# Loading batch 0 as token pairs and turning u of the first two batches on the tensor engine, in a fused retention and low-rank MLP kernel

## The chip, the cores and the metric

The kernel runs on one core of one Trainium2 chip. The metric is the device time in microseconds (us) of one execution; times are medians of the runs in the fast state. The engines are PE (matmul), DVE (vector), ACT (scalar), POOL (GpSimd) and SP (which here only issues loads). ACT and POOL issue DMAs too: ACT the transposing ones, POOL the weights and the stores.

## The reference, cut to what matters

```python
# q, k, v: (4 batches, 8 heads, 768 tokens, 64)
for t in range(S):                                  # retention, gamma per head
    state = gamma * state + k[:, :, t] (x) v[:, :, t]
    y[:, :, t] = scale * q[:, :, t] @ state
x  = y as (4, 768, 512)                             # heads side by side
u  = x + (x^T @ U @ V)^T                            # rank 32, along the tokens
out = u + relu(u @ w_ch1) @ w_ch2                   # 512 -> 2048 -> 512
```

The low-rank step mixes all 768 tokens of a batch, so u of a batch exists only when its whole attention is done. The MLP of batch b can start only then.

## The kernel before

The attention is computed in 128-token chunks with a state carried from chunk to chunk, in bf16. The matmuls of the MLP of batch b−1 are the carpet: they are issued in order, and pieces of the attention of batch b are woven in at marks, given as fractions of that MLP's cost.

```python
AT = {1: at(0.56, 0.052, 0.026), 2: at(0.09, 0.105, 0.05)}   # first chunk, step, score-to-mix
LR = {1: (0.87, 0.89, 0.905, 0.905), 2: (0.71, 0.75, 0.83, 0.89)}
for b in range(1, B):
    ...
    marks.append((s_at, part(score4, b, ci)))
    marks.append((m_at, part(mix4, b, ci)))
    ...
    marks += zip(LR[w], (mixed, part(lr_expand, b, 0, 4), part(lr_turn, b, 0),
                         part(lr_turn, b, 2)))
    weave(mlp_pieces(b - 1), marks)
```

The first MLP product needs u with the channels on the partitions (uT). `lr_turn` makes it, with DMAs that transpose, issued by ACT. (Only the first 512 tokens of batch 0 are made on PE directly.)

```python
def lr_turn(b, j0):
    for j in (j0, j0 + 1):
        nc.scalar.dma_start(out=uTs[b][:, :, ts(j, P)], in_=us[b][:, j],
                            transpose=True)
```

All loads of q, k and v go through SP in one fixed order. Batch 0 comes in 18 loads of 256 KB, one per tensor and 128-token chunk, in rows of 64 floats (256 B). After the gate below, which waits for the last w1 weights, the loads of the later batches follow.

```python
src[b, :, ts(ci, P), :].rearrange("h p d -> p h d")       # batch 0: 256 B packets
...
gate = rinT.tile([P, 2, NCK, 256], fp32, tag="kin", name="gate")
nc.gpsimd.tensor_copy(out=gate[:1, 0, 0, :1], in_=w1b[:1, 0, DH - 1:])
```

POOL casts the arrived tiles (`ki`, `qi`, `kd`, `vd`) and also issues the stores of the output, in program order. Three output tiles `o_sb` are in use in turn: DVE may write one only when the store of three tiles before has read it.

## Time and profile before

| | before |
|---|---|
| time, median | 263.67 us (263.1 to 264.25) |
| span of the profiled run, PE busy | 261.8 us, 224.0 us |
| first matmul of MLP 0 / 1 / 2 / 3 | 35.24 / 104.51 / 157.80 / 213.22 us |

From the profile's page: engine totals, then the busy tenths of PE and its granted clock in 40 slices of 6.5 us each, then the queue of the loads (q1) and of the transposes (q10) with packets, MB and share of the 16 DMA engines' time.

```profile
span 261.8 us, 5299 instructions
PE 224.0 (86%) x2224; PEld 120.4 (46%) x2224; DVE 102.6 (39%) x193; ACT 77.5 (30%) x172; POOL 95.1 (36%) x130
...
PE   0686789939999980999999996799999998999991
...
PEclk9999999988999997799999999799999999999997
...
q1 hardware_dynamic: 59520, 22.02, 44.9%
...
q10 hardware_dynamic: 10880, 2.62, 6.5%
```

PE is the engine that matters. It loses its time in the first five slices, in slice 9, in slice 16, and around slice 25, and PEclk drops behind the last three of these holes. The waits of PE in the timeline (start, length, line and operation, count, and in brackets the idle time before it with its releaser) say what the holes are:

```profile
35.24 3.15 PE L395 MATMUL mlp<-uT,w1b 128*128 128x512 bf16 x7 [0.68 <-ACT uT L75]
...
56.44 8.81 PE L395 MATMUL mlp<-uT,w1b 128*128 128x256 bf16 x64 [4.26 <-DMA uT<-u]
...
104.51 1.86 PE L395 MATMUL mlp<-uT,w1b 128*128 128x512 bf16 x4 [7.20 <-DMA uT<-u]
```

PE stood still for 4.26 and 7.20 us for transposes. The four 512-column matmuls after the second wait took 1.86 us, 0.47 each, where a warm one takes 0.22 (32 of them in 7.08 us from 45.10 us): half speed. The first line shows that the MLP begins at 35.24 us, also at half speed. (PEclk reads 9 there all the same, so this half speed is read from the durations alone.)

### The profile page before, as it was taken

Reading aid. Unit: us, or ns where it says so; the run is one execution under the profiler, and the core shown is the slowest. Engines: PE = TensorE matmul, PEld = TensorE weight load, DVE = VectorE, ACT = ScalarE, POOL = GpSimd, SP = SyncE. Lnnn points to the kernel's source line nnn. Section 1 sums busy time; section 2 is a strip of 40 time slices with the busy share of each in tenths; the row PEclk is TensorE's granted clock in tenths of the full one; section 3 lists DMA queues with packets and bytes.
Section 4 is the critical chain, followed back from the end, with each engine's and each line's share of the span. In section 5 each row is a group of like instructions: output and inputs, shape, how many; then the busy total and the mean of one; then the engine's idle time right before and its main releaser. Section 6 shows DMA issues by size and latency. Waiting matters only on the chain.

```text
span 261.8 us, 5299 instructions
## 1 busy us (share of the span) xinstructions
PE 224.0 (86%) x2224; PEld 120.4 (46%) x2224; DVE 102.6 (39%) x193; ACT 77.5 (30%) x172; POOL 95.1 (36%) x130
## 2 busy tenths in 40 slices
PE   0686789939999980999999996799999998999991
PEld 0475534428545430345754442346744443584440
DVE  5431324503465460466534501755543542331221
ACT  2555333415234200255541001256611013450000
POOL 4897900021993111979014436761000110000110
PEclk9999999988999997799999999799999999999997
DMA  8999999999919969889998189900002342001211
GB/s 163 218 210 172 174 192 217 238 196 201 191 43 208 269 119 189 165 223 171 206 211 138 54 170 256 245 3 5 3 4 78 106 125 52 0 0 44 80 66 54
DMA packets 77544, 35.72 MB, mean 136 GB/s; under 512 B 62544, under 2 KB 75984, under 8 KB 77520
## 3 DMA queue, kind: packets, MB, share of 16 engines
q1 hardware_dynamic: 59520, 22.02, 44.9%
q0 software_dynamic: 7120, 10.73, 17.5%
q10 hardware_dynamic: 10880, 2.62, 6.5%
q8 instruction: 17, 0.28, 0.5%
q14 instruction: 7, 0.06, 0.1%
HBM read 30.90 MB, written 6.29 MB: 142 GB/s over the span
## 4 chain that ended last, share of the span: by engine, by line
PE 33%; issue 31%; DMA 13%; SPq 6%; DVE 6%; POOL 6%; ACTq 3%; ACT 1%; POOLq 0%; DVEq 0%
PE mlp L395 15%; PE mlp L418 10%; DMA uT<-u 8%; SPq L133 6%; DMA in<-in_v_dram 4%; ACTq L376 3%; POOL out_dram L384 2%; DVE u L369 2%; PE r L334 2%; DMA out_dram<-o 2%; PE r L301 2%; DVE a L307 1%; PE r L325 1%; POOL vd L88 1%; PE st L286 1%
## 5 line engine op out<-in xcount | busy, mean ns | idle before, releaser
L395 PE MATMUL mlp<-uT,w1b 128*128 128x512 bf16 (+1 forms) x512 | 94.6, 341 | 17.3 <-DMA uT<-u 12.5
L418 PE MATMUL mlp<-w2b,gT 128*128 128x512 bf16 x384 | 88.0, 380 | 0.0
L395 PEld LDWEIGHTS <-w1b 128*128 128x128 bf16 x512 | 50.2, 101 | 54.0 <-issue 17.7
L402 ACT ACTIVATE gT<-mlp 128x512 bf16<-128x512 f32 (+1 forms) x88 | 42.4, 490 | 101.4 <-PE mlp L395 93.3
L418 PEld LDWEIGHTS <-gT 128*128 128x128 bf16 x384 | 35.5, 98 | 40.1
L384 POOL DMA_DIRECT2D out_dram<-o x24 | 13.4, 558 | 79.6 <-DVE o L423 79.6
L400 DVE TENSOR_SCALAR gT<-mlp 128x512 bf16<-128x512 f32 (+1 forms) x40 | 22.2, 555 | 44.2 <-PE mlp L395 44.0
L423 DVE TENSOR_TENSOR o<-mlp,u 128x512 f32<-128x512 f32 x24 | 16.6, 690 | 47.3 <-PE mlp L418 34.6
L307 DVE TENSOR_TENSOR a<-r,mask 128x512 bf16<-128x512 f32 x36 | 23.2, 686 | 17.2 <-PE r L301 15.4
L88 POOL TENSOR_TENSOR qi<-qin,gqT 128x512 bf16<-128x512 f32 x18 | 18.8, 1047 | 20.4 <-DMA qin<-in_q_dram 20.4
L86 POOL CAST ki<-kin 128x512 bf16<-128x512 f32 x18 | 13.5, 762 | 30.0 <-DMA kin<-in_k_dram 30.0
L88 POOL TENSOR_TENSOR vd<-in,gk 128x512 bf16<-128x512 f32 x18 | 18.6, 1040 | 14.1 <-DMA in<-in_v_dram 12.3
L369 DVE TENSOR_TENSOR u<-r,x 128x512 bf16<-128x512 f32 (+1 forms) x16 | 14.5, 951 | 14.7 <-PE r L362 14.7
L75 ACT ACTIVATE x<-r 128x256 bf16<-128x256 f32 x36 | 11.9, 381 | 27.4 <-PE r L334 25.6
L501 DVE TENSOR_TENSOR a<-r,mask 128x512 bf16<-128x512 f32 x12 | 7.7, 687 | 16.1 <-PE r L496 16.1
L75 ACT ACTIVATE qkT<-qk 128x1024 bf16<-128x1024 bf16 x6 | 6.1, 1024 | 10.8 <-PE qk L472 10.8
L86 POOL CAST kd<-in 128x512 bf16<-128x512 f32 x12 | 7.3, 610 | 4.2 <-DMA in<-in_k_dram 3.9
L470 PE MATMUL qk<-ident,qd 128*128 128x128 bf16 x24 | 3.7, 310 | 5.7 <-DVE ident L179 5.7
L301 PE MATMUL r<-qT,kT 32*128 32x128 bf16 x288 | 7.4, 221 | 0.9 <-DVE qT L251 0.9
L251 DVE STREAM_TRANSPOSE kT<-ki 128x256 f32<-128x256 f32 x18 | 7.8, 436 | 0.0
L251 DVE STREAM_TRANSPOSE qT<-qi 128x256 f32<-128x256 f32 x18 | 7.3, 406 | 1.0 <-POOL qi L88 1.0
L88 POOL TENSOR_TENSOR qd<-in,gq 128x512 bf16<-128x512 f32 x6 | 6.3, 1058 | 3.2 <-DMA in<-in_q_dram 3.2
(68 smaller groups left out, 129.2 us busy)
## 6 DMA issues: line engine op xcount, KB each, us to landing
in<-in_v_dram SPq DMA_DIRECT2D x24, 256.0 KB, 5.4
out_dram<-o POOLq DMA_DIRECT2D x24, 256.0 KB, 2.6
in<-in_k_dram SPq DMA_DIRECT2D x18, 256.0 KB, 5.2
kin<-in_k_dram SPq DMA_DIRECT2D x12, 384.0 KB, 7.7
qin<-in_q_dram SPq DMA_DIRECT2D x12, 384.0 KB, 12.1
w1b<-in_moe_w_ch_dram POOLq DMA_DIRECT2D x4, 512.0 KB, 8.1
w2b<-in_moe_w_ch_dram POOLq DMA_DIRECT2D x4, 512.0 KB, 17.3
in<-in_q_dram SPq DMA_DIRECT2D x6, 256.0 KB, 5.3
```

What stands on the lines that cost most here:

```text
L75: nc.scalar.activation(dst, src, AF.Copy)
L86: e.tensor_copy(out=dst, in_=src)
L88: e.tensor_tensor(dst, src, scale, op=ALU.mult)
L133: nc.sync.dma_start(out=t.rearrange("p (h d) -> p h d", h=H), in_=src)
L307: nc.vector.tensor_tensor(a[:, ds(4 * g, 4)].rearrange("p (n i) m -> p n i m", n=2), R[g][:, :, :256].rearrange("p n (i m) -> p n i m", i= ...
L369: nc.vector.tensor_tensor(v4(us[b][:, ds(j0, nj), e]), R[g][:, :, :nj * P].rearrange("p c (j e) -> p c j e", j=nj), v4(xs[b][:, ds(j0, nj) ...
L384: nc.gpsimd.dma_start(out=dst, in_=src)
L395: nc.tensor.matmul(g_p[:, :sz], w1b[:, c, ts(m, P)], uTs[b][:, c, ds(lo, sz)], start=(c == 0), stop=(c == NCB - 1))
L400: nc.vector.tensor_relu(gT[:, m, ds(lo, sz)], g_p[:, :sz])
L402: nc.scalar.activation(gT[:, m, ds(lo, sz)], g_p[:, :sz], AF.Relu)
L418: nc.tensor.matmul(ch, gT[:, m, ts(j, P)], w2b[:, m], start=(m == 0), stop=(m == NM - 1))
L423: nc.vector.tensor_tensor(o_sb, ch, us[b][:, j], op=ALU.add)
```

## The change

It has three parts:

1. *The start.* Batch 0 is loaded in blocks of 256 tokens, two neighbouring tokens in one row of 128 floats (packets of 512 B). Each block is worked as two chunks of 128 tokens (64 pairs) on the two halves of the partitions. Constants that only batch 1 needs are made later.
2. *The turns.* u of batches 0 and 1 is turned on PE (a matmul with the identity) and copied out by ACT; batches 2 and 3 keep the DMA.
3. *The marks.* Batch 1's attention and low-rank step are put later in MLP 0 and closer together, because the DMA's latency no longer has to be covered (10.0 to 12.6 us from issue to landing for the two transposes of batch 0's u, in the kernel before).

```diff
+    def load_early(nm, B0):
+        src = {"q": q, "k": k, "v": v}[nm][0, :, ds(256 * B0, 256), :].rearrange(
+            "h (t j) d -> t h (j d)", j=2)
+        ...                                   # k, q: one DMA of 512 KB; v: two of 256 KB
...
     def lr_turn(b, j0):
-        for j in (j0, j0 + 1):
-            nc.scalar.dma_start(out=uTs[b][:, :, ts(j, P)], in_=us[b][:, j],
-                                transpose=True)
+        if b > 1:
+            for j in (j0, j0 + 1):
+                nc.scalar.dma_start(out=uTs[b][:, :, ts(j, P)], in_=us[b][:, j],
+                                    transpose=True)
+            return
+        r = R[j0 // 2 % 2]
+        for c in range(NCB):
+            for jj in range(2):
+                nc.tensor.matmul(r[:, c // 2, ds(256 * (c % 2) + P * jj, P)],
+                                 us[b][:, j0 + jj, ts(c, P)], ident, start=True,
+                                 stop=True)
+        evac("A", uTs[b][:, :, ds(j0 * P, 2 * P)],
+             r.rearrange("p n (c t) -> p (n c) t", c=2))
...
-    with tc.tile_pool(name="psum0", bufs=1, space=bass.MemoryType.PSUM) as psum0:
-        ...                                   # six chunks: prep_first, turn0, mix0, score0
+    cast_early("k", 0, "DD")                  # D, P: on DVE, on POOL
+    cast_early("q", 0, "PD")
+    turn_early("k", 0)
+    turn_early("q", 0)
+    cast_early("v", 0, "PP")
+    ...                                       # three blocks, score_early, state_early, mix_early
+    cast_early("v", 2, "PD")
+    ...
+    late_consts()
...
-    AT = {1: at(0.56, 0.052, 0.026), 2: at(0.09, 0.105, 0.05)}
-    LR = {1: (0.87, 0.89, 0.905, 0.905), 2: (0.71, 0.75, 0.83, 0.89)}
+    AT = {1: at(0.74, 0.028, 0.014), 2: at(0.09, 0.105, 0.05)}
+    LR = {1: (0.91, 0.93, 0.95, 0.965), 2: (0.71, 0.75, 0.83, 0.89)}
```

More of the change, by code (lines that the diff above doesn't have):

```diff
@@ L39 @@
     RING = 19
-    NST = 4
+    NST = 3
     NLO = LO // P
@@ L59 @@
     BANKS = {"st": 1, "mlp": 3}
-    R = [psum.tile([P, 2, 512], fp32, tag="r0", name="r0")]
+    R = [psum.tile([P, 2, 512], fp32, tag=f"r{g}", name=f"r{g}") for g in range(2)]
     def bank(tag, dtype=fp32):
         n_bank[0] += 1
-        if tag in ("qk", "o"):
-            return psum0.tile([P, 2048 // (4 if dtype == fp32 else 2)], dtype,
-                              tag=tag, name=f"{tag}_{n_bank[0]}", bufs=1)
         return psum.tile([P, 2048 // (4 if dtype == fp32 else 2)], dtype,
@@ L101, in feed_natural @@
     def feed_natural(nm, b, ci):
-        src = {"q": q, "k": k, "v": v}[nm]
+        src = {"k": k, "v": v}[nm]
         feed.append(((nm, b, ci),
@@ L137, in take @@
         return ready.pop(key)
-    for ci in range(NCK):
-        for nm in "qkv":
-            feed_natural(nm, 0, ci)
     for b in range(1, B):
@@ L147 @@
             feed_natural("v", b, ci)
-    pos = consts.tile([P, NCK, H], fp32)
-    nc.gpsimd.iota(pos, pattern=[[P, NCK], [0, H]], base=0, channel_multiplier=1,
-                   allow_small_or_imprecise_dtypes=True)
-    srange = consts.tile([P, 1], fp32)
-    nc.gpsimd.iota(srange, pattern=[[0, 1]], base=0, channel_multiplier=1,
-                   allow_small_or_imprecise_dtypes=True)
-    jmat = consts.tile([P, P], fp32)
-    nc.gpsimd.iota(jmat, pattern=[[1, P]], base=0, channel_multiplier=0,
-                   allow_small_or_imprecise_dtypes=True)
+    NB = S // 256
@@ new lines @@
+    early = {}
+    kin0 = rinT.tile([P, NB, H, P], fp32, tag="kin", name="kin_0")
+    qin0 = rinT.tile([P, NB, H, P], fp32, tag="qin", name="qin_0")
+    def load_early(nm, B0):
+        src = {"q": q, "k": k, "v": v}[nm][0, :, ds(256 * B0, 256), :].rearrange(
+            "h (t j) d -> t h (j d)", j=2)
+        if nm == "v":
+            early["v", B0] = []
+            for f in range(2):
+                t = rin.tile([P, 4, P], fp32, tag="in", name=f"v0_{B0}_{f}")
+                nc.sync.dma_start(out=t, in_=src[:, ds(4 * f, 4)])
+                early["v", B0].append(t)
+        else:
+            t = (kin0 if nm == "k" else qin0)[:, B0]
+            nc.sync.dma_start(out=t, in_=src)
+            early[nm, B0] = [t[:, ds(4 * f, 4)] for f in range(2)]
@@ new lines, with ramp @@
+    for nm, B0 in ("k0", "q0", "v0", "k1", "q1", "k2", "q2"):
+        load_early(nm, int(B0))
+    n_ramp = [0]
+    def ramp(shape, pattern, mult):
+        n_ramp[0] += 1
+        t = consts.tile(shape, fp32, name=f"ramp{n_ramp[0]}")
+        nc.gpsimd.iota(t, pattern=pattern, base=0, channel_multiplier=mult,
+                       allow_small_or_imprecise_dtypes=True)
+        return t
+    srange = ramp([P, 1], [[0, 1]], 1)
+    jmat = ramp([P, P], [[1, P]], 0)
+    ident = consts.tile([P, P], bf16)
@@ new lines @@
+    nc.vector.tensor_scalar(ident, jmat, srange, None, op0=ALU.is_equal)
+    lg = [math.log(g) for g in gammas]
+    lgt = consts.tile([P, H], fp32)
+    for h in range(H):
+        nc.vector.memset(lgt[:, h:h + 1], lg[h])
+    pos2 = ramp([P, NB, H, 2], [[256, NB], [0, H], [1, 2]], 2)
+    nc.vector.tensor_tensor(
+        pos2, pos2, lgt[:, None, :, None].to_broadcast([P, NB, H, 2]), op=ALU.mult)
+    gq2 = consts.tile([P, NB, H, 2], fp32)
+    nc.scalar.activation(gq2, pos2, AF.Exp)
+    gk2 = consts.tile([P, NB, H, 2], fp32)
@@ new lines @@
+    nc.scalar.activation(gk2, pos2, AF.Exp, scale=-1.0)
+    nc.vector.tensor_scalar(gq2, gq2, 1.0 / math.sqrt(D), None, op0=ALU.mult)
+    jm2 = ramp([P, 2, P], [[-1, 2], [1, P]], 0)
+    s2 = ramp([P, 1], [[0, 1]], 2)
+    nc.vector.tensor_scalar(s2[ds(64, 64)], s2[ds(64, 64)], -128.0, None, op0=ALU.add)
+    mask2 = consts.tile([P, 2 * P], bf16)
+    nc.vector.tensor_scalar(mask2, jm2.rearrange("p j q -> p (j q)"), s2, None,
+                            op0=ALU.is_ge)
+    pos = ramp([P, NCK, H], [[P, NCK], [0, H]], 1)
@@ L159, with late_consts @@
                    channel_multiplier=4, allow_small_or_imprecise_dtypes=True)
-    feed_more()
-    lg = [math.log(g) for g in gammas]
-    for h in range(H):
-        nc.vector.tensor_scalar(pos[:, :, h], pos[:, :, h], lg[h], None,
-                                op0=ALU.mult)
-    gq = consts.tile([P, NCK, H], fp32)
-    nc.scalar.activation(gq, pos, AF.Exp)
-    gk = consts.tile([P, NCK, H], fp32)
-    nc.scalar.activation(gk, pos, AF.Exp, scale=-1.0)
-    nc.vector.tensor_scalar(gq, gq, 1.0 / math.sqrt(D), None, op0=ALU.mult)
-    for h in range(H):
-        r = ds(32 * (h // 2), 32)
-        nc.vector.tensor_scalar(
-            posT[r, :, h % 2], posT[r, :, h % 2],
-            -0.5 * math.log(D) / lg[h] - 128.0 * (h // 2), lg[h],
-            op0=ALU.add, op1=ALU.mult)
-    gqT = consts.tile([P, NCK, 2, 4], fp32)
-    nc.scalar.activation(gqT, posT, AF.Exp)
-    ident = consts.tile([P, P], bf16)
-    nc.vector.tensor_scalar(ident, jmat, srange, None, op0=ALU.is_equal)
-    mask = consts.tile([P, P], bf16)
-    nc.vector.tensor_scalar(mask, jmat, srange, None, op0=ALU.is_ge)
     states = []
     for i in range(NST):
-        t = consts.tile([P, 4, P], bf16, name=f"state{i}")
+        t = outp.tile([P, 4, P], bf16, tag="o_sb", name=f"state{i}")
         nc.vector.memset(t, 0.0)
         states.append(t)
+    mask = consts.tile([P, P], bf16)
+    gk = consts.tile([P, NCK, H], fp32)
+    gqT = consts.tile([P, NCK, 2, 4], fp32)
+    def late_consts():
+        nc.vector.tensor_scalar(mask, jmat, srange, None, op0=ALU.is_ge)
+        nc.vector.tensor_tensor(
+            pos, pos, lgt[:, None, :].to_broadcast([P, NCK, H]), op=ALU.mult)
+        nc.scalar.activation(gk, pos, AF.Exp, scale=-1.0)
+        for h in range(H):
+            r = ds(32 * (h // 2), 32)
+            nc.vector.tensor_scalar(
+                posT[r, :, h % 2], posT[r, :, h % 2],
+                -0.5 * math.log(D) / lg[h] - 128.0 * (h // 2), lg[h],
+                op0=ALU.add, op1=ALU.mult)
+        nc.scalar.activation(gqT, posT, AF.Exp)
     def causal(n):
@@ L450, in part @@
         return lambda: f(*args)
-    def prep_first(ci):
-        for nm, tag, g in (("q", "qi", gq), ("k", "kd", gk), ("v", "vd", None)):
-            t = rpre.tile([P, H, D], bf16, tag=tag, name=f"{nm}d_0_{ci}")
-            src = take(nm, 0, ci).rearrange("p (h d) -> p h d", h=H)
-            if g is not None:
-                g = g[:, ci, :, None].to_broadcast([P, H, D])
-            cast("P", t, src, g)
-            pre[nm, 0, ci] = t
-            feed_more()
-    n_state = [0]
-    def turn0(ci):
-        qd, kd, vb = (pre.pop((nm, 0, ci)) for nm in "qkv")
-        tp = bank("qk", bf16)
-        qkT = rmid.tile([P, 8, P], bf16, tag="a4", name=f"qkT_{ci}", bufs=3)
-        for p in range(4):
-            nc.tensor.transpose(tp[:, ts(p, P)], qd[:, ds(2 * p, 2)], ident)
-        for p in range(4):
-            nc.tensor.transpose(tp[:, ts(4 + p, P)], kd[:, ds(2 * p, 2)], ident)
-        evac("A", qkT, tp.rearrange("p (n m) -> p n m", n=8))
-        before = live.get("state0")
-        if ci < NCK - 1:
-            if ci == 0:
-                live["st_p", 0] = bank("st")
-            st_p = live["st_p", 0]
-            for p in range(4):
-                nc.tensor.matmul(st_p[:, ts(p, P)], kd[:, ds(2 * p, 2)],
-                                 vb[:, ds(2 * p, 2)],
-                                 start=(ci == 0 and p == 0), stop=True,
-                                 skip_group_check=True)
-            ns = states[n_state[0] % NST]
-            n_state[0] += 1
-            for i in range(2):
-                r = ds(D * i, D)
-                evac("A", ns[r, :, r], four(st_p)[r, :, r])
-            live["state0"] = ns
-        live[0, ci] = [vb, qkT, before]
@@ L492, in score0 @@
-    def score0(ci):
-        vb, qkT, state = live[0, ci]
-        for h in range(H):
-            r = ds(D * (h % 2), D)
-            nc.tensor.matmul(R[0][:, h % 2, ts(h // 2, P)], qkT[r, 4 + h // 2],
-                             qkT[r, h // 2], start=True, stop=True)
-        for i in range(2):
-            a = rpre.tile([P, 4, P], bf16, tag=("kT", "qT")[i],
-                          name=f"a{i}_0_{ci}")
-            nc.vector.tensor_tensor(a, four(R[0][:, i]), causal(4), op=ALU.mult)
-            live[0, ci].append(a)
@@ L504, in mix0 @@
-    def mix0(ci):
-        vb, qkT, state, *a = live.pop((0, ci))
-        o_p = bank("o")
-        if ci:
-            for p in range(4):
-                nc.tensor.matmul(o_p[:, ts(p, P)], qkT[:, p], state[:, p],
-                                 start=(p == 0), stop=False,
-                                 skip_group_check=True)
-        for i in range(2):
-            for h in range(i, H, 2):
-                nc.tensor.matmul(o_p[:, ts(h, D)], a[i][:, h // 2], vb[:, h],
-                                 start=(ci == 0 and h == 0), stop=True,
-                                 skip_group_check=True)
-        evac("A", xs[0][:, ci], o_p)
@@ L519 @@
-    xT = {}
-    def x_turn(j, cs):
-        for c in cs:
-            if c not in xT:
-                xT[c] = bank("mlp" if c < 3 else "qk")
-            nc.tensor.matmul(xT[c][:, ts(j, P)], xs[0][:, j, ts(c, P)], ident,
-                             start=(j == 0), stop=False, skip_group_check=True)
-    with tc.tile_pool(name="psum0", bufs=1, space=bass.MemoryType.PSUM) as psum0:
-        open_x(0)
-        prep_first(0)
-        for ci in range(NCK):
-            turn0(ci)
-            if ci + 1 < NCK:
-                if ci == NCK - 2:
-                    load_w1(0)
-                    load_w1(1)
-                prep_first(ci + 1)
-                if ci == 0:
-                    load_u()
-                elif ci < 3:
-                    load_v(2 * ci - 2)
-                    load_v(2 * ci - 1)
-            if ci > 0:
-                mix0(ci - 1)
-            score0(ci)
-            if 0 < ci <= NLO:
-                x_turn(ci - 1, range(3))
-        load_w1(2)
-        load_w1(3)
-        for j in range(4):
-            load_w2(j)
-        gate = rinT.tile([P, 2, NCK, 256], fp32, tag="kin", name="gate")
-        nc.gpsimd.tensor_copy(out=gate[:1, 0, 0, :1], in_=w1b[:1, 0, DH - 1:])
-        n_cast[0] = 2 * NCK
-        feed_more()
-        for j in range(NLO):
-            x_turn(j, (3,))
-        mix0(NCK - 1)
-        lr_open(0)
-        p_p = bank("o")
-        for j in range(NCK):
@@ new lines, in home, with cast_early @@
+    def home(shape, name):
+        return rin.tile(shape, bf16, tag="in", name=name)
+    eb = {}
+    def cast_early(nm, B0, engines):
+        t = eb[nm, B0] = home([P, 2, H, D], f"{nm}b_{B0}")
+        g = {"q": gq2, "k": None, "v": gk2}[nm]
+        for f in range(2):
+            hs = ds(4 * f, 4)
+            scale = None
+            if g is not None:
+                scale = g[:, B0, hs].rearrange("p h j -> p j h")
+                scale = scale[:, :, :, None].to_broadcast([P, 2, 4, D])
+            cast(engines[f], t[:, :, hs],
+                 early[nm, B0][f].rearrange("p h (j d) -> p j h d", j=2), scale)
@@ new lines, in turn_early @@
+    def turn_early(nm, B0):
+        src = eb[nm, B0]
+        tp = bank("mlp", bf16)
+        for hp in range(4):
+            for j in range(2):
+                nc.tensor.transpose(tp[:, ts(2 * hp + j, P)],
+                                    src[:, j, ds(2 * hp, 2)], ident)
+        t = eb[nm + "T", B0] = home([P, 4, 2 * P], f"{nm}t_{B0}")
+        dst = t
+        if nm == "q":
+            dst = t.rearrange("p n (t j) -> p n j t", j=2)
+        else:
+            dst = t.rearrange("p n (j t) -> p n j t", j=2)
+        evac("A", dst, tp.rearrange("p (n j t) -> p n j t", n=4, j=2))
@@ new lines, in score_early @@
+    def score_early(B0):
+        kT, qT = eb.pop(("kT", B0)), eb["qT", B0]
+        for g in range(2):
+            for n in range(2):
+                for j in range(2):
+                    for cc in range(2):
+                        for i in range(2):
+                            r = ds(64 * i, 64)
+                            nc.tensor.matmul(
+                                R[g][ds(64 * cc, 64), i, ts(2 * n + j, P)],
+                                kT[r, 2 * g + n, ds(128 * j + 64 * cc, 64)],
+                                qT[r, 2 * g + n, ts(cc, P)], start=True, stop=True)
+            a = eb["a", B0, g] = home([P, 4, 2 * P], f"a{g}_{B0}")
+            nc.vector.tensor_tensor(
+                a, R[g].rearrange("p i (n m) -> p (i n) m", n=2),
+                mask2[:, None, :].to_broadcast([P, 4, 2 * P]), op=ALU.mult)
@@ new lines, in state_early @@
+    def state_early(ci):
+        B0, r = ci // 2, ds(64 * (ci % 2), 64)
+        if ci == 0:
+            live["st_p", 0] = bank("st")
+        st_p = live["st_p", 0]
+        for j in range(2):
+            for h in range(H):
+                nc.tensor.matmul(st_p[ds(64 * (h % 2), 64), ts(h // 2, D)],
+                                 eb["k", B0][r, j, h], eb["v", B0][r, j, h],
+                                 start=(ci == 0 and j == 0 and h < 2), stop=True,
+                                 skip_group_check=True)
+        ns = states[ci % NST]
+        for i in range(2):
+            ri = ds(D * i, D)
+            evac("A", ns[ri, :, ri],
+                 st_p[ri, :256].rearrange("p (n m) -> p n m", n=4))
+        live["state", 0, ci] = ns
@@ new lines, in query_early, with mix_early @@
+    def query_early(ci, o_p):
+        if ci == 0:
+            return
+        ns = live.pop(("state", 0, ci - 1))
+        for hp in range(4):
+            nc.tensor.matmul(o_p[:, ts(hp, P)],
+                             eb["qT", ci // 2][:, hp, ts(ci % 2, P)], ns[:, hp],
+                             start=(hp == 0), stop=False, skip_group_check=True)
+    def mix_early(B0, engines="AA"):
+        o = [bank("mlp") for _ in range(2)]
+        for cc in range(2):
+            query_early(2 * B0 + cc, o[cc])
+        for g in range(2):
+            a = eb["a", B0, g]
+            for n in range(2):
+                for i in range(2):
+                    h = 4 * g + 2 * n + i
+                    for j in range(2):
+                        for cc in range(2):
+                            r = ds(64 * cc, 64)
+                            nc.tensor.matmul(
+                                o[cc][:, ts(h, D)], a[r, 2 * i + n, ts(j, P)],
+                                eb["v", B0][r, j, h],
+                                start=(2 * B0 + cc == 0 and h == 0 and j == 0),
+                                stop=True, skip_group_check=True)
+        for cc in range(2):
+            evac(engines[cc], xs[0][:, 2 * B0 + cc], o[cc])
+        for key in (("a", B0, 0), ("a", B0, 1), ("qT", B0), ("v", B0), ("k", B0)):
+            del eb[key]
@@ new lines, in xT, with x_turn @@
+    def xT(c):
+        return R[c // 2][:, c % 2]
+    def x_turn(c, js):
+        for j in js:
+            nc.tensor.matmul(xT(c)[:, ts(j, P)], xs[0][:, j, ts(c, P)], ident,
+                             start=(j == 0), stop=False, skip_group_check=True)
+    open_x(0)
+    lr_open(0)
+    cast_early("k", 0, "DD")
[3 more added lines that the diff above has]
+    cast_early("v", 0, "PP")
+    load_u()
+    cast_early("k", 1, "DD")
+    load_early("v", 1)
+    state_early(0)
@@ new lines @@
+    score_early(0)
+    state_early(1)
+    turn_early("k", 1)
+    cast_early("q", 1, "PP")
+    for c in range(NCB):
+        load_v(c)
+    mix_early(0)
+    cast_early("k", 2, "DD")
+    load_early("v", 2)
+    turn_early("q", 1)
+    cast_early("q", 2, "PD")
+    score_early(1)
+    turn_early("k", 2)
+    turn_early("q", 2)
+    cast_early("v", 1, "PP")
+    load_w1(0)
+    state_early(2)
+    state_early(3)
+    score_early(2)
+    mix_early(1)
+    cast_early("v", 2, "PD")
+    for mb in range(1, 4):
+        load_w1(mb)
@@ L562, with proj @@
+    p_p = bank("mlp")
+    def proj(js):
+        for j in js:
             for c in range(NCB):
@@ L565 @@
                                  stop=(j == NCK - 1))
-        pcs[0] = rmid.tile([P, P], bf16, tag="pc", name="pc_0")
-        evac("D", pcs[0], p_p[:, :P])
-        for c in range(NCB):
-            nc.tensor.matmul(xT[c][:, :LO], pcs[0][ds(RK * c, RK)],
-                             V4[ds(RK * c, RK), :LO], start=False, stop=True,
-                             skip_group_check=True)
-        for c in range(NCB):
-            evac("AD"[c % 2], uTs[0][:, c, :LO], xT[c][:, :LO])
-    psum1 = ctx.enter_context(
-        tc.tile_pool(name="psum1", bufs=1, space=bass.MemoryType.PSUM))
-    R.append(psum1.tile([P, 2, 512], fp32, tag="r1", name="r1"))
+    state_early(4)
+    proj(range(4))
+    mix_early(2, "DA")
+    for c in range(NCB):
+        x_turn(c, range(NLO))
+    proj(range(4, NCK))
+    pcs[0] = rmid.tile([P, P], bf16, tag="pc", name="pc_0")
+    evac("D", pcs[0], p_p[:, :P])
+    for c in (0, 2, 1, 3):
+        nc.tensor.matmul(xT(c)[:, :LO], pcs[0][ds(RK * c, RK)],
+                         V4[ds(RK * c, RK), :LO], start=False, stop=True,
+                         skip_group_check=True)
+    for c in range(NCB):
+        evac("AD"[c // 2], uTs[0][:, c, :LO], xT(c)[:, :LO])
+    late_consts()
+    for j in range(4):
+        load_w2(j)
+    gate = rinT.tile([P, 2, NCK, 256], fp32, tag="kin", name="gate")
+    nc.gpsimd.tensor_copy(out=gate[:1, 0, 0, :1], in_=w1b[:1, 0, DH - 1:])
+    n_cast[0] = 2 * NCK
+    feed_more()
     for ci in range(3):
```

## The prediction

> **What bounds it now.** PE is busy 224 of 261.8 us (the page); nearly all the rest is lost in four places (timeline, waits of PE).
> 1. Start: the first MLP matmul issues at 35.2 us. Batch 0 arrives in 256 KB pieces, one per about 1.2 us (218 GB/s, DMA saturated); POOL's vd cast of the last chunk waits for v until 23.5 us. PE runs at half speed here (a 512-column matmul takes 0.43 us at 35 us, 0.22 us later).
> 2. 4.3 us before 56.4 us: PE waits for the DMA transposes uT<-u, asked for at 42.3 us. The 64 matmuls after it take 8.8 instead of about 7.1 us (granted clock 0.72 to 0.81).
> 3. 7.2 us before 104.5 us: the same for batch 1's u; the next 20 matmuls lose about 1.9 us running slow.
> 4. Some 5 us in 147 to 167 us: DMA transposes of batch 2, batch 3's v late, stores stuck behind POOL casts.
>
> **What the change does.**
> - Batch 0 loads: 18,432 packets of 256 B become 9,216 of 512 B. [...] Estimate from 1.2 us per 1,024 short packets: 1.7 to 2.1 us per 512 KB, so v's last block lands at about 19 to 21 us rather than 23.5.
> - Then compute sets the start, not DMA. Per 256-token block: ACT 2 turns of 1.0, state copies 4x0.38, x 2x0.6 = 4.7 us; DVE about 4.3 us; POOL 3 to 4 us; PE 5 to 6 us at half speed. The last block's DVE half of the v cast sits behind both masks. Chaining these durations in program order I get the first MLP matmul between 31 and 36 us: 0 to 4 us gained. The denser PE work may bring the full clock before the MLP starts (about 1.7 us;[...] the trace's first 4 us of MLP agree).
> - w1 is asked for earlier (about 20 us against 24 to 28), lands at about 34 instead of 40.2 us, so batch 1's q arrives near 59 instead of 65 us.
> - u of batches 0 and 1 on PE: 8 matmuls (0.5 us) plus an ACT copy of about 1.1 us per pair of chunks, four times. It removes losses 2 and 3 (4.3+1.7+7.2+1.9 = 15 us) at a cost of 2 us PE and perhaps 2 us waiting for DVE's u (2.35 us).
> - Batch 1's attention is squeezed: 0.028 of the MLP (1.2 us) per chunk instead of 2.2 us. Score, mask (1.3 us), mix, x copy make about 3.3 us per chunk; PE has 2.6 us. About 4 us of new idle, against 1 us now.
> - DVE's posT scalings (1.8 us) now sit at the MLP's start: about 1 us.
>
> **Sum.** Start -2.5, loss 2 -6, loss 3 -9, PE turns and their waits +4, squeeze +3, late constants +1, slow clock at start -1.5: about -11 us. The rest shifts as a whole.
>
> Predicted 252.5 us, 8 in 10 within 246 to 259. Faster by over 2%: 0.85; within 2%: 0.13; slower: 0.02.
>
> **What would show it.** First MLP matmul at 31 to 36 us; no wait for uT before 100 us; MLP 1's first matmul at 93 to 97 us (now 104.5); waits of score/mix for DVE masks and ACT x of 3 to 5 us in 63 to 88 us.
>
> **What would make it wrong.** PE staying at half speed through the start (then 38 us or later); w2 or batch 1's q late; batch 2's loads, gated by batch 1's casts, not moving forward with PE, so that the gain is given back after 100 us.

The sum: −2.5 −6 −9 +4 +3 +1 −1.5 = −11 us. Two estimates of mine: the 1.7 to 2.1 us per 512 KB (part of the start's −2.5), which lie between 1.2 us, if the time went by the packet, and 2.4 us, if it went by the byte; and that denser PE work brings the full clock earlier (the −1.5). For the second there was only the trace of the kernel before, where the MLP's first seven matmuls took 3.15 us (0.45 each) and the 24 from 39.08 us took 5.76 us (0.24 each).

## More of the kernel before

The waits of SP, which issues the loads, in the first 110 us (total, times, longest):

```profile
SPq L133 <- DMA uT<-u: 16.8, 5, 8.8
...
SPq L114 <- DMA uT<-u: 3.2, 1, 3.2
```

SP too waited 20 us for transposes of u, although what it was about to issue were loads of the next batch, which read nothing of u.

## The result, and the profile after

| | before | after |
|---|---|---|
| time, median | 263.67 us | 251.94 us (250.89 to 252.88) |
| span, PE busy | 261.8, 224.0 us | 249.7, 219.3 us |
| first matmul of MLP 0 | 35.24 us | 32.48 us |
| MLP 0, first matmul to that of MLP 1 | 69.3 us | 60.3 us |
| MLP 1, likewise | 53.3 us | 51.4 us |
| MLP 2, likewise | 55.4 us | 56.5 us |

The ratio of the two is 0.9554, with a 95% interval of 0.9507 to 0.9601. (Ratios here are the mean time of one kernel's fast runs over the mean of the other's fast runs of the same rounds, so not quite the ratio of the medians.)

The page of the changed kernel, the same lines:

```profile
span 249.7 us, 5671 instructions
PE 219.3 (88%) x2412; PEld 121.3 (49%) x2412; DVE 105.8 (42%) x200; ACT 81.6 (33%) x176; POOL 89.7 (36%) x124
...
PE   1577889999978879999999965999999998999990
...
PEclk9999999999999999999999997999999999999999
...
q1 hardware_dynamic: 50208, 22.02, 43.9%
...
q10 hardware_dynamic: 6528, 1.57, 3.3%
```

The load queue moved the same 22.02 MB in 9,312 fewer packets. Its share hardly fell only because the span is shorter too. The timeline of PE, at the places that answer to those of before, and a fourth one:

```profile
32.48 2.16 PE L438 MATMUL mlp<-uT,w1b 128*128 128x512 bf16 x8 [0.74 <-ACT uT L72]
...
45.83 9.09 PE L438 MATMUL mlp<-uT,w1b 128*128 128x512 bf16 x73
...
92.78 1.02 PE L438 MATMUL mlp<-uT,w1b 128*128 128x512 bf16 x4 [0.25 <-ACT uT L72]
...
152.45 1.43 PE L438 MATMUL mlp<-uT,w1b 128*128 128x512 bf16 x4 [3.77 <-DVE o L466]
...
155.20 2.68 PE L438 MATMUL mlp<-uT,w1b 128*128 128x512 bf16 x8
```

The MLP starts 2.8 us earlier, and its first eight matmuls take 0.27 us each instead of 0.45, against 0.22 for a warm one. In MLP 0 there is no wait for uT, and at the start of MLP 1 one of 0.25 us. But in MLP 2 PE waits 3.77 us for DVE and then runs slow (0.34 us per matmul at 155 us). This hole was 2.4 us before, and it has grown. SP's waits between 120 and 145 us:

```profile
SPq L130 <- DMA uT<-u: 14.4, 4, 9.6
...
SPq L130 <- DMA qin<-in_q_dram: 4.6, 3, 1.6
```

The 20 us of waits of SP for transposes before 110 us are gone, as batches 0 and 1 have none. Those for batch 2's transposes are still there. SP does not run free before 110 us, though: its list for that stretch has 20.8 us of other waits at the line of the k and v loads (L130), put down to PE, ACT and DVE, the longest 4.6 us. No run looked into them. The first k load of batch 2 still went out earlier, at 78.94 instead of 97.72 us.

### The profile page after: what moved, and what is told of

Read it like the earlier page. It is cut to its first block, busy times and chain, and to the rows that moved or that the text cites. A ratio compares the mean times of both kernels' runs of the same rounds, so it can differ in the third digit from the quotient of the medians.

```text
span 249.7 us, 5671 instructions
## 1 busy us (share of the span) xinstructions
PE 219.3 (88%) x2412; PEld 121.3 (49%) x2412; DVE 105.8 (42%) x200; ACT 81.6 (33%) x176; POOL 89.7 (36%) x124
## 3 DMA queue, kind: packets, MB, share of 16 engines
q1 hardware_dynamic: 50208, 22.02, 43.9%
## 4 chain that ended last, share of the span: by engine, by line
PE 39%; issue 32%; DMA 8%; DVE 7%; SPq 5%; POOL 3%; ACT 2%; ACTq 1%; POOLq 0%; DVEq 0%
PE mlp L438 19%; PE mlp L461 11%; DMA out_dram<-o 3%; SPq L158 3%; POOL out_dram L427 2%; DVE a L340 2%; SPq L154 2%; DMA v<-in_v_dram 2%; DVE u L402 2%; PE r L367 2%; PE r L334 1%; DVE o L466 1%; DMA in<-in_v_dram 1%; PE r L358 1%; DMA uT<-u 1%
## 5 line engine op out<-in xcount | busy, mean ns | idle before, releaser
L438 PE MATMUL mlp<-uT,w1b 128*128 128x512 bf16 (+1 forms) x512 | 89.7, 328 | 7.2 <-DVE o L466 3.8
L438 PEld LDWEIGHTS <-w1b 128*128 128x128 bf16 x512 | 48.5, 98 | 39.8 <-issue 9.2
L443 DVE TENSOR_SCALAR gT<-mlp 128x512 bf16<-128x512 f32 (+1 forms) x40 | 22.1, 553 | 37.1 <-PE mlp L438 37.1
L340 DVE TENSOR_TENSOR a<-r,mask 128x512 bf16<-128x512 f32 x36 | 23.2, 686 | 16.4 <-PE r L334 14.5
L85 POOL TENSOR_TENSOR qi<-qin,gqT 128x512 bf16<-128x512 f32 x18 | 18.7, 1045 | 21.5 <-DMA qin<-in_q_dram 21.5
L85 POOL TENSOR_TENSOR vd<-in,gk 128x512 bf16<-128x512 f32 x18 | 18.6, 1038 | 8.8 <-DMA in<-in_v_dram 7.0
L541 DVE TENSOR_TENSOR a<-r,mask 128x1024 bf16<-128x1024 f32 x6 | 7.1, 1220 | 4.2 <-ACT state L72 3.1
L358 PE MATMUL r<-ns,qT 32*128 32x64 bf16 x240 | 5.4, 191 | 3.5 <-DVE a L340 3.5
L518 PE MATMUL mlp<-ident,kb 128*128 128x128 bf16 x24 | 3.1, 311 | 5.4 <-DVE kb L83 5.4
L367 PE MATMUL r<-vd,a 128*128 128x64 bf16 x144 | 7.5, 194 | 0.3 <-DVE a L340 0.3
L72 ACT ACTIVATE uT<-r 128x1024 bf16<-128x1024 f32 (+1 forms) x6 | 5.2, 879 | 7.7 <-PE r L416 5.9
L334 PEld LDWEIGHTS <-kT 32*128 32x128 bf16 x288 | 4.5, 94 | 6.5 <-issue 4.0
```

The source lines that it names most:

```text
L72: nc.scalar.activation(dst, src, AF.Copy)
L85: e.tensor_tensor(dst, src, scale, op=ALU.mult)
L334: nc.tensor.matmul(R[hp // 2][:, hp % 2, ts(i, P)], turned("kT", b, ci, i, c, r), turned("qT", b, ci, i, c, r), start=(c == 0), stop=(c == 1))
L340: nc.vector.tensor_tensor(a[:, ds(4 * g, 4)].rearrange("p (n i) m -> p n i m", n=2), R[g][:, :, :256].rearrange("p n (i m) -> p n i m", i= ...
L438: nc.tensor.matmul(g_p[:, :sz], w1b[:, c, ts(m, P)], uTs[b][:, c, ds(lo, sz)], start=(c == 0), stop=(c == NCB - 1))
L443: nc.vector.tensor_relu(gT[:, m, ds(lo, sz)], g_p[:, :sz])
```

## The experiments

Twelve kernels were run, each beside the kernel before on the same chip. All gave correct results. Those named `before_...` are edits of the kernel before, the others of the changed one. Runs 1 to 4 share one chip and its runs of before (264.03 us), so do runs 5 to 8 (263.6 us) and 9 to 12 (263.25 us).

The theory at the outset was that of the prediction: the PE turns remove two waits of PE and their cold clock, and the new start gives a smaller part, set by compute and no longer by loads. The rivals were that the packets alone make the start, that the marks make the gain, and that the turns act through something other than PE's own waits.

### 1. before_pe_turn: only the turns

Edit: the `lr_turn` of the diff above, in the kernel before.

> Kernel before, with only u of batches 0 and 1 turned on PE. My theory (waits for the DMA transposes and the load queue held up behind them are the larger half of the gain): the start stays at 35.2 us, no wait for uT before 110 us, but PE now reaches batch 1's attention mark about 5 us before q has landed and waits 2 to 4 us there; 256 to 258 us, ratio about 0.975. Rival (the gain is the shorter start with 512-byte loads, which moves the whole load schedule): 261 us or more, ratio over 0.99.

Measured: 257.66 us, ratio 0.9757 (0.9683 to 0.9831). The turns alone give 6 us, about half of the change. The two waits for uT that I had costed at 15 us with their cold clock are gone, but PE finds the next thing to wait for, in the timeline of this run:

```profile
65.91 0.62 PE L301 MATMUL r<-qT,kT 32*128 32x128 bf16 x16 [4.51 <-DVE qT L251]
```

It had run ahead to batch 1's attention, whose q was still on its way (its loads start after the w1 weights).

### 2. after_dma_turn: the change without the PE turns

```diff
     def lr_turn(b, j0):
-        if b > 1:
+        if b > -1:
```

> Changed kernel, with u of all batches turned by DMA again. My theory: the start stays at 32.5 us; PE waits 3 to 5 us for batch 0's transposes and 6 to 8 us for batch 1's, both followed by slow matmuls; 259 to 264 us. Rival (the start and the new order carry the gain): 255 us or less.

Measured: 270.54 us, ratio 1.0232 (1.0169 to 1.0294): slower than the kernel before. All expectations were too low. From its timelines, of SP and then of PE:

```profile
78.52 24.96 SPq L111 DMA_DIRECT2D qin<-in_q_dram  x4
```

```profile
110.30 1.87 PE L438 MATMUL mlp<-uT,w1b 128*128 128x512 bf16 x4 [9.31 <-DMA uT<-u]
```

PE waits 9.31 us, more than the 7.20 of before (and 5.61 us for batch 0's turns, where it was 4.26). And SP takes 25 us to issue the four loads of batch 2's q; its list of waits has 18.7 us of one wait for `uT<-u` in there. After a gap of 2.07 us in MLP 0 the granted clock was 0.53 from 90 to 96 us as well. Is it the new start or the late marks? Run 11 tells.

### 3. after_256: the new start with short packets

The same blocks in the same tiles, but each load is split into its even and odd tokens.

```diff
-            nc.sync.dma_start(out=t, in_=src)
+            for jj in range(2):
+                nc.sync.dma_start(out=t[:, :, ds(64 * jj, 64)],
+                                  in_=src[:, :, ds(64 * jj, 64)])
```

> Changed kernel, same layout and work, but each batch 0 load split in two loads of 256-byte pieces. My theory (the start is set by compute more than by loads, with about 2 us to spare): v's last block lands 4 to 5 us later (about 24 to 25 us instead of 20), the first MLP matmul 2 to 3 us later (34.5 to 35.5), total 254 to 255 us. If loads alone set the start: 4 to 5 us later, 256 to 257 us. If compute alone: under 1 us.

Measured: 256.32 us, ratio 0.9698 (0.9624 to 0.9773), so 4.4 us over the changed kernel. The timelines, DVE's scaling of the last block's q (it waits for the load) and the first MLP matmul, in the changed kernel and then in this run:

```profile
16.07 0.69 DVE L85 TENSOR_TENSOR qb<-qin,gq 128x512 bf16<-128x512 f32 x1 [1.18 <-DMA qin<-in_q_dram]
```

```profile
21.99 0.69 DVE L85 TENSOR_TENSOR qb<-qin,gq 128x512 bf16<-128x512 f32 x1 [3.37 <-DMA qin<-in_q_dram]
...
37.35 2.16 PE L442 MATMUL mlp<-uT,w1b 128*128 128x512 bf16 x8 [0.74 <-ACT uT L72]
```

The last q comes 5.9 us later and the MLP starts 4.9 us later (37.35 against 32.48; 4.3 to 6.1 with the scatter that run 5 tells of). So the start follows the loads, which my own theory (2 to 3 us) denied. With short packets the new start would even be 2.1 us later than the old one (37.35 against 35.24): the work in blocks alone gains nothing here, and the packets are what pays. One caution: the run also issues twice as many loads for batch 0.

### 4. after_b0_only: u of batch 0 alone on PE

```diff
-        if b > 1:
+        if b > 0:
```

> Changed kernel, with only batch 0's u on PE, batch 1's by DMA as in the kernel before. My theory: MLP 0 unchanged, PE waits about 7 us for batch 1's transposes and runs about 2 us slow afterwards, less about 3 us of PE turns and their waits: 257 to 259 us. Rival: within 2 us of the changed kernel.

Measured: 258.53 us, ratio 0.979 (0.9719 to 0.9861), as expected. PE waited 9.2 us before MLP 1 and ran at half speed after (0.47 us per matmul, granted clock 0.50 from 98 to 103 us; the profile names a load of k as the releaser, but these matmuls read uT). SP waited for transposes again (12.8 and 9.6 us in the first 110 us). So of the 18.6 us that lie between run 2 and the changed kernel, batch 0's turn brings 12.0 and batch 1's 6.6, taken in this order.

### 5. after_fill: fillers to warm PE from the beginning

24 matmuls of 512 columns that nothing reads, put into the waits of the start.

```diff
+    def fill(n):
+        for _ in range(n):
+            nc.tensor.matmul(R[1][:, 1], ident,
+                             ident[:, None, :].to_broadcast([P, 4, P]),
+                             start=True, stop=True)
...
+    fill(7)
     cast_early("k", 0, "DD")
```

> Changed kernel with 24 extra matmuls (512 columns, result unused) put into PE's idle places of the first 27 us, to raise PE's clock early. If PE at half speed sets the stretch from batch 0's last q to the MLP: 128-column turns drop from 0.13 to under 0.08 us each before 20 us, and the first MLP matmul comes at 29 to 31 us instead of 32.5; the total gains less, 1 to 2 us (250 to 251), since batch 1's q still lands at 59. If ACT, DVE or the loads set it: first MLP matmul within 0.5 us of 32.5.

Measured: 254.15 us, ratio 0.9618 (0.9568 to 0.9668). PE did get its full speed early, but it did not keep it, and the MLP started at 33.27 us, no earlier than without the fillers. From PE's timeline:

```profile
17.13 0.62 PE L518 MATMUL mlp<-ident,kb 128*128 128x128 bf16 x8
...
19.91 0.25 PE L552 MATMUL st<-vb,kb 64*64 64x64 bf16 x4 [1.63 <-POOL vb L85]
...
33.27 2.16 PE L438 MATMUL mlp<-uT,w1b 128*128 128x512 bf16 x8 [0.74 <-ACT uT L72]
```

The turns take 0.62 us for eight, where cold ones take 1.03 (the changed kernel's, at 18.17 us), and PE waits for the cast of v instead. So before 20 us PE's half speed does not set the start: with run 3, the loads and the casts behind them do. For the rest of the start this run tells nothing. Behind the wait of 1.63 us PE fell back (29 score matmuls took 1.08 us from 23.00 us, where 32 had taken 0.64 at 16.56) and did so again at the end (the 16 turns of x took 1.89 us from 29.58), and three of the fillers stand in the critical chain themselves (1.39 us from 21.29 us).

Other traces do tell something. The nine traces of this start without this edit or that of run 3 (the changed kernel and runs 2, 4, 6 to 10 and 12) scale the last q at 16.0 to 16.2 us, but begin the MLP between 31.21 and 33.02 us. Here are PE's 16 turns of x, just before it, in the earliest (run 4) and in the latest (run 8):

```profile
28.38 1.07 PE L599 MATMUL r<-ident,x 128*128 128x128 bf16 x16
```

```profile
29.26 1.89 PE L599 MATMUL r<-ident,x 128*128 128x128 bf16 x16
```

The start is earliest where PE runs fast in its last 5 us. So PE's speed there goes with up to 1.8 us of the start; this is a comparison of traces, and no run was made for it.

### 6. after_wide: batch 1's attention less squeezed

```diff
-    AT = {1: at(0.74, 0.028, 0.014), ...
+    AT = {1: at(0.66, 0.042, 0.021), ...
```

> Changed kernel with batch 1's attention spread wider (from 0.66 in steps of 0.042 instead of 0.74 in steps of 0.028). My theory (the squeeze costs PE about 3.8 us of waits for DVE's masks): those waits fall to under 1.5 us, 249.5 to 251 us. Rival (the wait only moves to q or v of batch 1, which have not landed): waits for qT or vd of 2 us or more, 252 us or more.

Measured: 250.96 us, ratio 0.9516 (0.9486 to 0.9545). The waits of PE for DVE's masking fell from 3.5 to 1.7 us, and MLP 1 started at 91.08 instead of 92.78 us. The squeeze cost 1.7 us up to there. Of the whole time it is 1 us, within what runs scatter.

### 7. after_b2_pe: u of batch 2 on PE as well

```diff
-        if b > 1:
+        if b > 2:
```

> Changed kernel with u of batch 2 on PE as well. My theory (the transposes also hold up the loads behind them: the load queue waited 9.6 us for them, v of batch 3 came late, POOL's stores stood behind its cast, and MLP 2 waited 3.8 us for an output buffer): these waits go, MLP 2's waits of 5 us near 144 to 152 us fall under 1.5 us, at a cost of about 2.5 us of PE turns and their waits; 248.5 to 250.5 us. Rival (that stall has another cause): 252 to 254 us.

Measured: 245.83 us, ratio 0.932 (0.929 to 0.9351), 6 us under the changed kernel and clearly below what I expected. PE's own wait for batch 2's uT had been only 0.75 us. The gain is in MLP 2: from its first matmul to that of MLP 3 it takes 51.0 us (143.58 to 194.61) instead of 56.5. The waits of SP for transposes and the wait of PE for DVE's o are gone. The chain between them can be read in POOL's timeline of the changed kernel:

```profile
134.82 0.61 POOL L83 CAST kd<-in 128x512 bf16<-128x512 f32 x1
141.47 1.04 POOL L85 TENSOR_TENSOR vd<-in,gk 128x512 bf16<-128x512 f32 x1 [6.04 <-DMA in<-in_v_dram]
142.45 0.58 POOL L427 DMA_DIRECT2D out_dram<-o  x1
```

and of this run:

```profile
134.47 0.61 POOL L83 CAST kd<-in 128x512 bf16<-128x512 f32 x1
135.04 1.04 POOL L85 TENSOR_TENSOR vd<-in,gk 128x512 bf16<-128x512 f32 x1
136.02 0.58 POOL L427 DMA_DIRECT2D out_dram<-o  x1
```

With the transposes, POOL waits 6.04 us for a load of batch 3's v that came late, and the store behind it goes out 6.4 us later. The rest is in the chain of the changed kernel (`--critical`; start, length, what):

```profile
135.62 2.52 DMA uT<-u
138.16 3.18 DMA in<-in_v_dram
...
142.45 2.99 DMA out_dram<-o
...
145.57 0.69 DVE o L466
146.26 5.32 DMA out_dram<-o
...
151.70 0.69 DVE o L466
```

DVE can write its o at 145.57 us only when the late store has landed. The next store goes out at 146.26 us, behind more of POOL's casts, and takes 5.32 us to land. DVE waits 5.44 us for it, and PE for DVE. Why the load was late, SP's timeline of the changed kernel shows:

```profile
126.91 1.65 SPq L130 DMA_DIRECT2D in<-in_k_dram  x1
138.16 0.37 SPq L130 DMA_DIRECT2D in<-in_v_dram  x1
```

SP stood still for 9.6 us, for a transpose that ACT issued only at 135.62 us, 7 us after SP had begun to wait. In this run the loads go out one after another in that stretch.

### 8. after_old_marks: the change without the new marks

```diff
-    AT = {1: at(0.74, 0.028, 0.014), ...
-    LR = {1: (0.91, 0.93, 0.95, 0.965), ...
+    AT = {1: at(0.56, 0.052, 0.026), ...
+    LR = {1: (0.87, 0.89, 0.905, 0.905), ...
```

> Changed kernel with the marks of the kernel before for batch 1's attention and its low-rank step. My theory: PE reaches the attention 4 to 6 us before batch 1's q and waits for it, the waits for DVE's masks fall to about 1 us, and the rest is the same; 253 to 255.5 us. Rival (the marks make no difference): within 1 us of the changed kernel.

Measured: 254.12 us, ratio 0.9605 (0.955 to 0.966). With the early marks PE waits 4.42 us at 62.70 for batch 1's q, and MLP 1 starts at 95.48 instead of 92.78 us (0.5 us of this is the scatter of the start, 33.02 against 32.48). With the turns on PE the late marks are worth 1 to 2 us of the time (1.3 by the ratios, 2.2 by the medians), and the intervals overlap.

### 9. after_b2_ghost: transposes that nothing reads

Is it the hold-up of SP, or was it PE's wait and the cold clock that run 7 removed? This kernel is run 7 with batch 2's six transposes issued as well, at their old places, into tiles that nothing reads.

```diff
+        if b == 2:
+            for j in (j0, j0 + 1):
+                gh = ghosts.tile([P, NCB, P], bf16, tag="ghost", name=f"ghost{j}")
+                nc.scalar.dma_start(out=gh, in_=us[b][:, j], transpose=True)
         r = R[j0 // 2 % 2]
```

> As after_b2_pe (245.83 us: u of batches 0, 1 and 2 turned on PE), with the six DMA transposes of batch 2's u issued as well, at their old places on the Activation queue, into six tiles that nothing reads. PE cannot wait for them; what they can still do is hold up what stands behind them on the load queue. Theory 'the transposes cost time through the loads behind them on the SP queue': waits of SP for these transposes of 9 to 15 us come back around 100 to 160 us, the v loads and o wait of MLP 2 come back, and the kernel takes 248 to 250.5 us. Rival 'the gain of after_b2_pe was PE's own wait and half-speed time behind the last transpose': 245 to 247 us, with SP's waits back or not but no longer span.

Measured: 252.42 us, ratio 0.9573 (0.9529 to 0.9617). The whole gain of run 7 is lost (251.94 us was the changed kernel; I had said 248 to 250.5). SP's waits from 120 to 150 us, then PE's timeline:

```profile
SPq L131 <- DMA ghost<-u: 16.6, 4, 11.0
```

```profile
149.21 1.02 PE L443 MATMUL mlp<-uT,w1b 128*128 128x512 bf16 x4 [1.80 <-DVE o L471]
152.70 1.21 PE L421 MATMUL r<-ident,u 128*128 128x128 bf16 x8 [2.46 <-DVE u L403]
153.70 3.62 PE L443 MATMUL mlp<-uT,w1b 128*128 128x512 bf16 x8
```

SP waits for DMAs whose results nobody uses, so this is no dependence on data. POOL's v cast waits 7.3 us for its load, DVE 10.8 us for its output tile, and PE loses 4.3 us in two waits and then runs at half speed (3.62 us for eight). The theory of the hold-up stands, and the rival (245 to 247 us) falls. The loss lies in MLP 2, which takes 57.9 us (144.61 to 202.54) against 51.0 in run 7. The late v load went out at 138.64 us, where run 7 issued it at 128.60, and had landed when POOL's cast began at 141.93 us: it is the issue that is late, not the transfer. The run also adds the transposes' own traffic and their issue on ACT, so not all of its 6.6 us over run 7 (on another chip) need be SP's wait.

### 10. after_b2_wide: runs 6 and 7 together

Edit: the edits of runs 6 and 7.

> after_b2_pe (245.83) with the wider marks of after_wide for batch 1's attention. If the two gains add (after_wide took MLP 1's start from 92.8 to 91.1 us; after_b2_pe acts from 100 us on): 244 to 245 us, faster than both kernels and than each single step. If the squeeze was only hidden slack that after_b2_pe had already used: 245.5 to 246.5.

Measured: 244.63 us, ratio 0.9273 (0.923 to 0.9316). This is the fastest kernel, 19 us under the kernel before and 7 us under the changed one. That it also beats run 7 (0.932) is likely but not shown, as the intervals overlap and the chips differ.

### 11. dma_turn_old_marks: the new start alone

Edit: run 2 with the marks of run 8.

> The block start of the changed kernel with every u turned by DMA (as after_dma_turn, 270.54) but with the marks of the kernel before (AT and LR of batch 1). Separates the late marks from the earlier start as the reason that after_dma_turn was 7 us slower than the kernel before. If the late marks did it: 259 to 263 us (4 us less than before is the start, less some extra wait). If the new start itself collides with the transposes (more k, q loads behind them): 266 to 271.

Measured: 260.46 us, ratio 0.9872 (0.9816 to 0.9929). The profiled execution fell into the slow state (326.54 us), so its trace is not used. The new start alone is worth 3 us, and it was the late marks that made run 2 slow, by some 10 us. The traces of run 2 and of the kernel before agree with this: ACT issues batch 1's first transposes at 100.71 instead of 95.31 us, PE waits 9.31 instead of 7.20 us for them, and SP 18.7 us in one wait, where the longest was 8.8.

### 12. after_all_pe: every batch on PE

```diff
-        if b > 1:
+        if b > 3:
```

> Every batch's u on PE, the marks of the kernel before for batch 1 (so compare with after_old_marks 254.12 for the start, and after_b2_pe 245.83 for the rest). Theory 'a PE turn pays where a transposed tile is waited for or loads stand behind it': batch 3 has no loads behind and its wait was small, so its turn costs PE 24 matmuls of 128 columns, some 1.3 to 2 us, and gains nothing: with the old marks' 2 us, 248 to 250.5. If PE turns pay everywhere: 247 or less.

The expectation describes the kernel wrongly: it has the marks of the changed kernel, not those of before, so it is to be compared with run 7 directly, and the numbers given there are 2 us too high. Measured: 246.66 us, ratio 0.9353 (0.9308 to 0.9399), and PE's last matmul ends 0.75 us after that of run 7. So the turn of batch 3, which nothing waits for and behind which no loads stand, gains nothing on PE; whether it costs something the intervals leave open.

## Why the prediction was right, and where it was wrong

The time (252.5 predicted, 251.94 measured) and the class were right. These are the steps of the sum:

- **Start, "−2.5".** Measured −2.76 (first MLP matmul) and 3 us of the time (run 11). The size was right, the reason only in part. The last two loads of v landed at about 20.7 and 22.1 us (19 to 21 predicted). "Then compute sets the start, not DMA" is the step that failed: with packets of 256 B the start moved by 4.9 us, nearly as much as the last load of q (5.9), so the loads had little to spare (run 3). Compute has its share too: 11.8 us pass between the last cast that PE waits for because of its load (20.69 us) and the MLP, and PE's speed in there goes with up to 1.8 us (run 5). My chain of durations gave 31 to 36 us, too wide to tell the two apart.
- **Packets.** That 512 KB would take 1.7 to 2.1 us was my estimate; the runs show it. Between 6 and 14 us, with the DMA engines busy throughout in all three (a DMA share of 1.21 to 1.41 in that view), the changed kernel moved 290 GB/s, which is 1.8 us per 512 KB, run 3 218 GB/s and the kernel before 215 GB/s. For batch 0 they issue 12, 24 and 18 loads, so the number of loads differs too.
- **Clock.** "The denser PE work may bring the full clock before the MLP starts" held: the first eight matmuls took 2.16 us, where seven took 3.15 us before. That denser work is the cause, no run shows apart for the start of the MLP; before 20 us, eight turns took 0.62 instead of 1.03 us with the fillers of run 5, which only add work. PE ran at half speed after waits of 4.26, 7.20 and 3.77 us: the granted clock was 0.50 from 57.5 to 60 and from 102 to 107.5 us in the kernel before, and from 153.5 to 156.2 us in the changed one. Shorter waits were followed by it too: in run 9 two waits of 1.80 and 2.46 us, with 1 us of matmuls between them, were followed by 0.45 us per 512-column matmul. Which wait is short enough, these runs do not show.
- **Losses 2 and 3, "−6" and "−9", turns "+4", squeeze "+3", late constants "+1", slow clock at the start "−1.5".** Summed for MLP 0 alone, with the 7.2 us of loss 3 and the three of the four turns that lie in it (+3), this is −6 −7.2 +3 +3 +1 −1.5 = −7.7 us; measured −9.0. The traces account for this: both waits are gone; the waits for masks are 3.8 us against 1.1 (+2.7); the turns take PE 1.35 us and 1.3 us of waits for u and uT (+2.7); the first eight matmuls are 1.4 us shorter. The term that did not come is the late constants: PE is busy in 27.4 of the first 27.5 us of MLP 0. MLP 1's first matmul came at 92.78 us, just before the 93 to 97 us that I gave.
- **MLP 1: the 1.9 us of slow matmuls.** Measured −1.9, with the fourth turn in it.
- **"The rest shifts as a whole."** Nearly: MLP 2 took 1.1 us more. PE arrived earlier, batch 2's transposes held SP as before, and the wait for o grew from 2.39 to 3.77 us. Loss 4 of the prediction names the late v and the stores behind POOL's casts, but not SP's wait, which makes the v late. MLP 3 took 0.4 us more.

That the total came within 0.6 us is partly luck: MLPs 0 and 1 gained some 2.3 us more than the terms said, MLPs 2 and 3 lost 1.5 us that the sum did not have.

One more thing is missing in the prediction: the turns also free SP's load queue from waits for transposes (runs 7 and 9 show what that is worth for batch 2). The measured effects of the parts show how much the parts depend on each other:

| turns of batches 0, 1 | old start, old marks | new start, old marks | new start, new marks |
|---|---|---|---|
| by DMA | 1 | 0.9872 | 1.0232 |
| on PE | 0.9757 | 0.9605 | 0.9554 |

With the old marks start and turns add up: 0.9872 × 0.9757 = 0.963, against 0.9605 measured. The new marks turn from a loss of some 10 us into a small gain when the transposes of these batches go. The prediction had them only as a cost (squeeze, +3); it did not see that they are a loss with the DMA turns alone.

In the trace it is SP's sequencer that stands still for these transposes, though ACT issues them: for up to 9.6 us in the changed kernel, and for 11.0 us for one whose result nothing reads (run 9). Why the loads wait for these transposes at all, when no data ties them, is not settled: the profile shows the wait and its releaser, and no run changed how semaphores are given out.

## What to carry to other kernels

Look at the waits of the queue that issues the loads, not only at those of the busiest engine: a wait there for a DMA of another kind, which the loads do not need, can cost several us half a batch later (up to 6 us here, by runs 7 and 9), through a cast, a store behind it and an output tile. Before moving work in time, ask which latency its present place covers; the late marks cost some 10 us with DMA turns and gained 1 to 2 with PE turns. And test a claim such as "compute sets this stage" by slowing the loads and by speeding up the compute, one at a time, and look in the trace whether the speeding up lasted: the fillers of run 5 warmed PE for the first 20 us only.
